# State products of a chunked recurrence in three column groups, next to the output products

## The chip, the cores and the metric

The kernel runs on one core of a Trainium2 chip. The metric is the device time of one execution in microseconds; three runs of the kernel before gave 1037.36, 1039.93 and 1042.68 us, so the median is 1039.93 us. The engines are named as in the profile: PE is TensorE's matrix products, PEld its weight loads, DVE is VectorE, ACT is ScalarE, POOL is GpSimd and SP issues most of the transfers.

## The reference

Three layers follow one another: a gated linear recurrence (4 sequences, 8 heads, 768 tokens, head width 48), a gated layer (`_moe_ref`) that computes `silu(xn @ w_gate) * (xn @ w_val) @ w_out` on normalized rows, and a layer of eight experts of which each token uses one. The change lies in the recurrence alone.

```python
def _attn_ref(q, k, v, a_re, a_im):
    ...
    for t in range(S):
        ar, ai = (a_re_n[:, :, t, :, None], a_im_n[:, :, t, :, None])
        new_re = ar * S_re - ai * S_im
        new_im = ar * S_im + ai * S_re
        kv = np.einsum('bhd,bhe->bhde', k[:, :, t], v[:, :, t])
        S_re, S_im = (new_re + kv, new_im)
        y[:, :, t] = np.einsum('bhd,bhde->bhe', q[:, :, t], S_re)
    return y

def reference(**kwargs):
    attn_out = _attn_ref(**attn_kwargs)
    B, H, S, D = attn_out.shape
    x = np.ascontiguousarray(attn_out.transpose(0, 2, 1, 3)).reshape(B * S, H * D)
    x = _moe_ref(x=x, **moe_kwargs)
    return _moe2_ref(x=x, **moe2_kwargs)
```

## The kernel before

The 3072 tokens are 24 chunks of 128. Two sequences take turns, so chunk i + 2 is the one that follows chunk i in its sequence, and a sequence is six chunks. The recurrence of a chunk runs in stages `s0` to `s10`. The factors of q and k (`QF`, `KF`; real and imaginary part side by side, 2 x 48 = 96 columns a head) are made in `s6`. `s7` transposes them (`ptQT`, `ptKT`, L663). `s8` makes the products of queries and keys (`pAT`, L680) and, unless the chunk is its sequence's last, the **state products** (`pKV`, L692): for each of 8 heads the stationary operand is `KF` (128 tokens x 96 columns), the moving operand is `V` (128 tokens x 48 columns), and the result is 96 x 48. DVE adds the old state (L697) and multiplies by the decay of the chunk (L699); the outcome, `Sn`, is read by `s9` of chunk i + 2. `s9` makes the **output products** `pyT` (L712 from `A` and `V`, L718 from `Sn` and `QT`): their results are 64 rows high and stand at rows 0 and 64 of the bank for even and odd heads, so that they already lie in two groups of 64 columns of TensorE. ACT copies them (`yT`, L725), PE transposes them back (`py`, L728), DVE normalizes (`XN`), and `s10` transposes again (`pxT`). The data of all these products are float32, and the trace shows each such product as two passes with a weight load each.

Beside the recurrence run the gated layer's products of the block of two or three chunks before: `pg` and `pv` (24 products of float32r with 256 or 384 moving columns for each f of 12), then `po` of the f before (L762 to L764). They fill most of PE's time.

The order of the work is written out by hand: a table of events with due times (`at`, `EARLY`, `NUDGE`, `SLOT`) sets the order in which the stages are called, and the scheduler of the framework then places each instruction in its engine's queue by that order and its own estimate of durations. Each engine runs its queue in order. Tiles come from pools with a fixed count of buffers: `KF` shares a tag of six (`r3`) with the other large tiles of the recurrence, `Sn` has three, `V` two, and the banks of `pAT`, `pKV`, `pyT`, `py` and the transposes are three (`bank`).

Of the kernel before, what the change touches and what calls it, by code (L numbers as in the profile page):

```python
# [115 lines left out]
def rsqrt(nc, y, x, a):  # L116
    """y = x ** -0.5, finite where x is 0; a is scratch"""
    nc.vector.tensor_scalar(y.bitcast(I32), x.bitcast(I32), 1, None, op0=ALU.logical_shift_right)
    nc.vector.tensor_scalar(y.bitcast(I32), y.bitcast(I32), -1.0, float(0x5F3759DF), op0=ALU.mult, op1=ALU.add)
    for _ in range(3):  # L120
        nc.vector.tensor_tensor(out=a, in0=y, in1=x, op=ALU.mult)
        nc.vector.scalar_tensor_tensor(out=a, in0=a, scalar=-0.5, in1=y, op0=ALU.mult, op1=ALU.mult)
        nc.vector.scalar_tensor_tensor(out=y, in0=a, scalar=1.5, in1=y, op0=ALU.add, op1=ALU.mult)


def inv_norm(nc, dst, ss, a):
    """dst = 1 / (sqrt(ss) + 1e-6); a is scratch"""
    rsqrt(nc, dst, ss, a)
    nc.vector.tensor_tensor(out=dst, in0=dst, in1=ss, op=ALU.mult)
    nc.vector.tensor_scalar(dst, dst, 1e-6, None, op0=ALU.add)  # L130
    nc.vector.reciprocal(dst, dst)
# [3 lines left out]
def general_path(tc, pools, H, q, k, v, are, aim, w64, g, w1, w2, out, ident, wE, enT):  # L135
    """the whole computation for inputs outside the ranges that the fast path is made for"""
    nc = tc.nc
# [78 lines left out]
    with tc.For_i(0, NT, P) as t0:  # L216
        def cols(x, name):
            """[token, feature] -> [feature, token]"""
            b = ps.tile([P, 512], F32, tag="a", name="gpt")
            for c in range(NC):  # L220
                nc.tensor.transpose(b[:, c * P:(c + 1) * P], x[:, c * P:(c + 1) * P], ident)
            t = gp.tile([P, NC, P], F32, tag=name, name=name, bufs=1)
            nc.scalar.activation(t, b[:, :DM].rearrange("p (c t) -> p c t", c=NC), AF.Copy)
            return t
# [71 lines left out]
def fused_kernel(ctx: ExitStack, tc: tile.TileContext, H, q, k, v, are, aim, wg, wv, wo, g, emb, tau, w1, w2, out):  # L296
# [67 lines left out]
    def apart(group, inst):  # L364
        """an indirect store whose rows no other one of the group writes"""
        tc.declare_no_dep(inst.ins, group=group, reason="each row is written once")
        tc.add_to_no_dep_group(group, inst.ins)
# [16 lines left out]
    def warm_up(n):  # L384
        """products of constants, so that TensorE is at its full clock when the first of the data comes"""
        b = psG.tile([P, BLK], F32, tag="g", name="warm")
        for _ in range(n):
            nc.tensor.matmul(b[:, :P], ones, ident, start=True, stop=True)
# [32 lines left out]

# [1 line left out]
    SETS = {  # L423
# [29 lines left out]

# [1 line left out]
    wop = ExitStack()  # L455
# [16 lines left out]
    def conv(n):  # L472
        """float64 to float32, and that to the two parts of the products"""
        _, dst, f = units[n]
# [12 lines left out]
    def check_weight(n):  # L487
        """the least magnitude of the upper words as float32, which tells of weights below the range of float32"""
        if n < len(units):
            hi = raw_t.pop(n)[:, :, 1].bitcast(F32)  # L490
            nc.vector.tensor_reduce(out=wmin[:, n:n + 1], in_=hi, axis=AX.X, op=ALU.min, apply_absolute_value=True)

    def check_re(n, load):
        """the least real part of the decay factors"""
        if load:
# [5 lines left out]

# [1 line left out]
    pap = ExitStack()  # L503
# [79 lines left out]
    def sums(i, part):  # L583
        """the sums of X over the tokens up to each one, in turns and in logarithms"""
        if i < PLAIN:
# [89 lines left out]
    def s8(i):  # L675
        for hf in range(2):
# [9 lines left out]
            st["A", i, hf] = A  # L686
        KF = st.pop(("KF", i))
        if not is_last(i):
            V, G = st["V", i], st.pop(("G", i))
            b = bank("pKV")  # L690
            for h in range(H):
                nc.tensor.matmul(b[:D2, h * D:(h + 1) * D], KF[:, h].rearrange("p z d -> p (z d)"), V[:, h * D:(h + 1) * D], start=True, stop=True)  # L692
            Sn = pa.tile([P, DM + HP - D], F32, tag="S", name="Sn", bufs=3)
            nc.gpsimd.memset(Sn[:, DM:], 0.0)
            kv = b[:D2, :DM]
            if not is_first(i):
                nc.vector.tensor_tensor(out=Sn[:D2, :DM], in0=kv, in1=st["S", i][:D2, :DM], op=ALU.add)  # L697
                kv = Sn[:D2, :DM]
            nc.vector.tensor_tensor(  # L699
                out=hd(Sn[:D2, :DM]), in0=hd(kv), in1=G[:D2].unsqueeze(2).broadcast_to([D2, H, D]), op=ALU.mult  # L700
            )
            st["S", i + 2] = Sn

    def s9(i):
        first = is_first(i)
        V = st.pop(("V", i))
        Sp = None if first else st.pop(("S", i))
# [48 lines left out]

# [1 line left out]
    def split_mm(o, lhs, rhs, start, stop):  # L758
        """o (+)= (lh + ll)^T (rh + rl) with the product of the small parts left to rounding"""
        n = len(lhs)  # L760
# [35 lines left out]

# [1 line left out]
    def e1(j):  # L798
# [7 lines left out]
    def e4(j, tl):  # L806
        """rows of a tile, the products with the embeddings beside them"""
        xs = st["x2", j]
# [78 lines left out]

# [1 line left out]
    def find_flag():  # L889
# [27 lines left out]

# [1 line left out]
    exr = ExitStack()  # L919
# [8 lines left out]
    def tiles(p):  # L928
        """the expert of a pass and the tiles of its slots"""
        e, lo, hi = PASSES[p]  # L930
        return e, range(lo // P, -(-hi // P))

    def rank_experts():
        """the experts by their tokens so far, the most first: the turn in which each is processed, and its slots"""
        pc = bank("pcount")[:, :E]
# [24 lines left out]
    def open_experts():  # L960
        """what the first expert needs early, in the place of the recurrence"""
        pap.close()
# [14 lines left out]
    def load_perm(room, last):  # L977
        """the tokens by turn and slot; a row up to the last one where there is none"""
        nc.sync.dma_start(out=perm, in_=perm_d.rearrange("(t p e) o -> p t (e o)", p=P, e=E))
# [10 lines left out]
    def head_perm():  # L990
        """of all blocks but the last one"""
        load_perm(moe.tile([P, DM], F32, tag="ct", name="room", bufs=CT_BUFS), rows(blocks[NB - 1][0] - 1).stop - 1)
# [18 lines left out]
    def load_raw(e, n):  # L1011
        """a half of w1 or of w2"""
        if e >= E:
# [10 lines left out]
    def split(e, n, part):  # L1024
        """half of a half of w1 or of w2, to the two parts of the products"""
        if e >= E:
# [14 lines left out]
    def xpose(p):  # L1041
        """the tokens of a pass, features first"""
        if p >= len(PASSES):
# [26 lines left out]
    def store(e, tl, n, src, gate):  # L1070
        """the rows of a tile, times their gates, to their places"""
        o = pool[1].tile([P, DM], F32, tag="o", name="o", bufs=4)
# [6 lines left out]
    def by_feature(e):  # L1079
        """where the last tile would hold few tokens, the outputs are made features first, for the tokens that there are"""  # L1080
        return 0 < CAPS[e] % P <= FLIP

    def ex_out(p, f, part=None):
        """the products with w2; of the last pass the last tile by itself, so that the others are stored meanwhile"""
        e, lo, hi = PASSES[p]
# [24 lines left out]
    def turn_back(p, f):  # L1110
        """the outputs of an expert, tokens first"""
        e, _, hi = PASSES[p]
# [35 lines left out]

# [1 line left out]
    uses = {s2: [AF.Ln, AF.Exp], s4: [AF.Arctan], s5: [AF.Exp, AF.Exp], s5b: [AF.Exp, AF.Exp], s6: [AF.Sin, AF.Sin], moe_g: [AF.Tanh], e5: [AF.Exp]}  # L1150
# [113 lines left out]
def _tokens(a):  # L1264
    """[batch, head, token, feature] -> [batch, token, head * feature]"""
    b, h, s, d = a.shape
# [3 lines left out]
def _columns(a):  # L1270
    """[row, column] -> [block of columns, row in block of rows, block of rows, column in block]"""
    r, c = a.shape
# [3 lines left out]
def _rows(a):  # L1276
    """[row, column] -> [block of rows, row in block, column]"""
    return a.reshape(-1, P, a.shape[1])
# [37 lines left out]
```

## Time and profile before

| | |
|---|---|
| median of three runs | 1039.93 us |
| the profiled execution, span | 1035.3 us |
| PE busy | 972.8 us (94%) |
| PEld busy | 931.2 us (90%) |
| DVE busy | 674.4 us (65%) |
| ACT busy | 609.3 us (59%) |
| POOL busy | 250.4 us (24%) |
| state products `pKV`, PE busy | 31.9 us in 320 passes |

The span reaches from the first to the last instruction of one execution; the median of the runs is 4.6 us longer than this span. A busy share is an average over stages: the recurrence and the gated layer run side by side up to about 740 us, the experts after that. TensorE's clock is granted at full speed (2.4 GHz) or at half (1.2 GHz); it is at half in several stretches between 40 and 170 us, and at full speed from there to the last few microseconds. Matrix products overlap, so a row of several passes is longer than the distance from its start to the start of the next row; this distance is what a group of passes costs.

### The profile page before, as it was taken

The numbers are of one execution on the slowest core, as the hardware profiler recorded it, in microseconds if no ns is written. First come the engines' busy times: TensorE is split into PE (matmuls) and PEld (weight loads), VectorE is DVE, ScalarE is ACT, GpSimd is POOL, SyncE is SP. The second block draws the span as 40 slices with busy tenths as digits, with TensorE's granted clock in tenths as the row PEclk, the third lists the DMA queues.
The fourth block names the chain that finished last, engine by engine and source line by source line (L and its number), as shares of the span: only waits on it lengthen the run. The fifth ranks groups of instructions, "written<-read, shape, count | busy, mean of one in ns | idle before, by whom it ended". The sixth has DMA issues, their size and how long they took to land.

```text
span 1035.3 us, 18190 instructions
## 1 busy us (share of the span) xinstructions
PE 972.8 (94%) x6729; PEld 931.2 (90%) x6729; DVE 674.4 (65%) x1618; ACT 609.3 (59%) x1106; POOL 250.4 (24%) x264
## 2 busy tenths in 40 slices
PE   5868788899999999999999999999988999999995
PEld 5867687899999999999999999999988999999995
DVE  6898997877766866866876776464557533444420
ACT  6565656767768767767776865542445433455531
POOL 4355653311211211221031120110104202322221
PEclk9897989999999999999999999999999999999998
DMA  6443441214311511611511331030235534554210
GB/s 198 132 138 102 139 127 48 47 40 135 51 40 53 163 39 47 192 39 40 170 54 40 106 106 36 18 99 1 73 97 186 159 106 148 178 176 161 92 38 23
DMA packets 75537, 99.24 MB, mean 96 GB/s; under 512 B 27327, under 2 KB 57502, under 8 KB 75440
## 3 DMA queue, kind: packets, MB, share of 16 engines
q1 hardware_dynamic: 70272, 87.30, 28.4%
q0 software_dynamic: 5168, 10.70, 3.1%
q8 instruction: 55, 0.90, 0.4%
q14 instruction: 42, 0.34, 0.1%
HBM read 88.04 MB, written 10.50 MB: 95 GB/s over the span
## 4 chain that ended last, share of the span: by engine, by line
PE 66%; issue 9%; DVE 4%; DMA 4%; POOL 3%; ACT 2%; SPq 0%; POOLq 0%; ACTq 0%; DVEq 0%
PE pg L762 4%; PE pv L762 4%; PE po L762 4%; PE pg L764 4%; PE pg L763 4%; PE pv L764 4%; PE pv L763 4%; PE po L763 4%; PE po L764 4%; PE pAT L680 3%; PE ph L762 3%; PE eo L762 3%; PE eo L763 3%; PE ph L764 3%; PE ph L763 3%
## 5 line engine op out<-in xcount | busy, mean ns | idle before, releaser
L762 PE MATMUL pg<-xth,wg 128*128 128x384 f32 (+1 forms) x324 | 109.2, 337 | 9.8 <-DVE th L777 9.8
L763 PE MATMUL po<-htl,wo 128*128 128x384 f32 (+1 forms) x324 | 105.9, 327 | 8.5 <-DVE htl L786 6.2
L438 ACT ACT_TABLE_LOAD x87 | 111.6, 1283 | 1.5
L762 PE MATMUL pv<-xth,wv 128*128 128x384 f32 (+1 forms) x324 | 107.5, 332 | 1.9 <-DVE th L783 1.9
L762 PE MATMUL po<-hth,wo 128*128 128x384 f32 (+1 forms) x324 | 106.9, 333 | 0.0
L763 PE MATMUL pg<-xtl,wg 128*128 128x384 f32 (+1 forms) x324 | 105.7, 326 | 0.0
L764 PE MATMUL pg<-xth,wg 128*128 128x384 f32 (+1 forms) x324 | 105.5, 326 | 0.0
L764 PE MATMUL pv<-xth,wv 128*128 128x384 f32 (+1 forms) x324 | 103.9, 321 | 0.4 <-POOL wv L484 0.4
L764 PE MATMUL po<-hth,wo 128*128 128x384 f32 (+1 forms) x324 | 104.2, 322 | 0.0
L763 PE MATMUL pv<-xtl,wv 128*128 128x384 f32 (+1 forms) x324 | 103.5, 319 | 0.0
L438 ACT ACTIVATE th<-pg 128x384 f32<-128x384 f32 (+1 forms) x108 | 49.0, 454 | 90.5 <-PE pg L764 89.6
L785 ACT ACTIVATE hth<-th 128x384 fp32r<-128x384 f32 (+1 forms) x108 | 52.5, 486 | 78.3 <-DVE th L783 72.2
L1068 DVE SCALAR_TENSOR_TENSOR hel<-ph,heh 128x256 fp32r<-128x256 f32 (+6 forms) x72 | 39.9, 554 | 89.7 <-ACT heh L1067 89.6
L777 DVE SCALAR_TENSOR_TENSOR th<-th,pg 128x384 f32<-128x384 f32 (+1 forms) x108 | 54.5, 505 | 47.5 <-ACT th L438 47.0
L1067 ACT ACTIVATE heh<-ph 128x256 fp32r<-128x256 f32 (+6 forms) x72 | 35.0, 486 | 74.7 <-PE ph L764 72.1
L1036 DVE TENSOR_TENSOR wl<-raw,wh 128x768 fp32r<-128x768 f32 x64 | 59.4, 954 | 29.0 <-ACT wh L1035 28.9
L786 DVE TENSOR_TENSOR htl<-th,hth 128x384 fp32r<-128x384 f32 (+1 forms) x108 | 60.5, 560 | 27.2 <-ACT hth L785 26.8
L762 PEld LDWEIGHTS pg<-xth,wg 128*128 128x128 f32 x324 | 63.0, 195 | 14.2 <-DVE th L777 11.9
L762 PE MATMUL ph<-xeh,wh 128*128 128x256 f32 (+6 forms) x216 | 75.1, 348 | 0.0
L764 PE MATMUL ph<-xeh,wl 128*128 128x256 f32 (+6 forms) x216 | 72.6, 336 | 0.0
L763 PE MATMUL ph<-xel,wh 128*128 128x256 f32 (+6 forms) x216 | 72.4, 335 | 0.0
L763 PEld LDWEIGHTS po<-htl,wo 128*128 128x128 f32 x324 | 62.3, 192 | 9.9 <-DVE htl L786 7.1
(252 smaller groups left out, 2689.0 us busy)
## 6 DMA issues: line engine op xcount, KB each, us to landing
raw<-in_moe_w_dram SPq DMA_DIRECT2D x32, 768.0 KB
raw<-in_moe_w_gate_dram SPq DMA_DIRECT2D x24, 384.0 KB
raw<-in_moe_w_val_dram SPq DMA_DIRECT2D x24, 384.0 KB
raw<-in_moe_w_out_dram SPq DMA_DIRECT2D x24, 384.0 KB
X<-in_a_im_dram SPq DMA_DIRECT2D x24, 192.0 KB
X<-in_a_re_dram SPq DMA_DIRECT2D x24, 192.0 KB
V<-in_v_dram SPq DMA_DIRECT2D x24, 192.0 KB
x2d<-row SPq DMA_DIRECT2D x24, 192.0 KB
```

Of the source, the lines that this page charges most:

```text
L438: chain[0] = fn(*args, **kw)
L680: nc.tensor.matmul(b[:, h * P:(h + 1) * P], KT[:D2, h], QT[:D2, h], start=True, stop=True)
L762: nc.tensor.matmul(o, lh, rh, start=start and x == 0, stop=False)
L763: nc.tensor.matmul(o, lh, rl, start=False, stop=False)
L764: nc.tensor.matmul(o, ll, rh, start=False, stop=stop and x == n - 1)
L777: nc.vector.scalar_tensor_tensor(out=t, in0=t, scalar=1.0, in1=b, op0=ALU.add, op1=ALU.mult)
L785: nc.scalar.activation(hh, t, AF.Copy)
L786: (nc.gpsimd if j < POOL_H else nc.vector).tensor_tensor(out=hl, in0=t, in1=hh.bitcast(F32), op=ALU.subtract)
L1036: nc.vector.tensor_tensor(out=dl, in0=rw, in1=dh.bitcast(F32), op=ALU.subtract)
L1067: nc.scalar.activation(hh, b, AF.Relu)
L1068: nc.vector.scalar_tensor_tensor(out=hl, in0=b, scalar=0.0, in1=hh.bitcast(F32), op0=ALU.max, op1=ALU.subtract)
```

## The change

`state` is a new function that holds the state products and what follows from them. It is called by `s9` of the same chunk, ahead of the output products, and no longer from `s8`. In it the 96 columns of `KF` are cut into three of 32, and each piece has a product of its own whose result stands at rows 0, 32 and 64 of the bank: 24 products of 32 x 48 a chunk where there were 8 of 96 x 48. Comments and docstrings are dropped, and later lines shift by nine.

```diff
@@ s8 @@
             st["A", i, hf] = A
-        KF = st.pop(("KF", i))
-        if not is_last(i):
-            V, G = st["V", i], st.pop(("G", i))
-            b = bank("pKV")
-            for h in range(H):
-                nc.tensor.matmul(b[:D2, h * D:(h + 1) * D], KF[:, h].rearrange("p z d -> p (z d)"), V[:, h * D:(h + 1) * D], start=True, stop=True)
-            Sn = pa.tile([P, DM + HP - D], F32, tag="S", name="Sn", bufs=3)
...
+    def state(i):
+        KF = st.pop(("KF", i)).rearrange("p h z d -> p h (z d)")
+        if is_last(i):
+            return
+        V, G = st["V", i], st.pop(("G", i))
+        b = bank("pKV")
+        for h in range(H):
+            for lo in range(0, D2, 32):
+                nc.tensor.matmul(
+                    b[lo:lo + 32, h * D:(h + 1) * D], KF[:, h, lo:lo + 32], V[:, h * D:(h + 1) * D],
+                    start=True, stop=True, skip_group_check=True,
+                )
+        Sn = pa.tile([P, DM + HP - D], F32, tag="S", name="Sn", bufs=3)
...
     def s9(i):
         first = is_first(i)
+        state(i)
         V = st.pop(("V", i))
```

The first place is PE's queue around the products of queries and keys of chunk 14 (about 434 us in the trace). Before:

```order
L764 MATMUL pg<-xth,wg_110 128x384
L680 MATMUL pAT<-QT,KT 128x128 x8
L692 MATMUL pKV<-V,KF 96x48 x8
L762 MATMUL pv<-xth,wv_111 128x384
L763 MATMUL pv<-xtl,wv_111 128x384
```

and after:

```order
L773 MATMUL pg<-xth,wg_110 128x384
L680 MATMUL pAT<-QT,KT 128x128 x8
L771 MATMUL pv<-xth,wv_111 128x384
L772 MATMUL pv<-xtl,wv_111 128x384
L773 MATMUL pv<-xth,wv_112 128x384
```

The state products are gone from here, and the gated layer's `pv` follows `pAT` at once. The second place is PE's queue around the output products of the same chunk (about 443 us). Before:

```order
L764 MATMUL pv<-xth,wv_112 128x384
L712 MATMUL pyT<-A,V 64x128 x2
L718 MATMUL pyT<-QT,Sn 64x128 x2
L712 MATMUL pyT<-A,V 64x128 x2
```

and after:

```order
L773 MATMUL pv<-xth,wv_112 128x384
L697 MATMUL pKV<-V,KF 32x48 x24
L721 MATMUL pyT<-A,V 64x128 x2
L727 MATMUL pyT<-QT,Sn 64x128 x2
L721 MATMUL pyT<-A,V 64x128 x2
```

The 24 small products now stand straight ahead of `pyT`, which itself is as it was. The third place is the end of the same output products, up to the transposes `py` that need ACT's copy of `pyT`. Before:

```order
L718 MATMUL pyT<-QT,Sn 64x128 x2
L762 MATMUL po_4818<-hth,wo_107 128x384
L763 MATMUL po_4818<-htl,wo_107 128x384
L764 MATMUL po_4818<-hth,wo_108 128x384
L762 MATMUL po_4819<-hth,wo_107 128x384
L763 MATMUL po_4819<-htl,wo_107 128x384
L764 MATMUL po_4819<-hth,wo_108 128x384
L762 MATMUL po_4820<-hth,wo_107 128x384
L728 MATMUL py<-beside,yT 128x128 x4
```

and after:

```order
L727 MATMUL pyT<-QT,Sn 64x128 x2
L771 MATMUL po_4982<-hth,wo_107 128x384
L772 MATMUL po_4982<-htl,wo_107 128x384
L773 MATMUL po_4982<-hth,wo_108 128x384
L771 MATMUL po_4983<-hth,wo_107 128x384
L737 MATMUL py<-beside,yT 128x128 x4
```

Where seven products of the gated layer stood between `pyT` and `py`, four stand now. Over the chunks from number 5 on the count is lower in nine of nineteen, the same in eight, and higher in two.

## Rows read from the trace of the kernel before

**Rows 1.** The page, part 1: engine, busy us (share of the span) xinstructions.

```profile
PE 972.8 (94%) x6729; PEld 931.2 (90%) x6729; DVE 674.4 (65%) x1618; ACT 609.3 (59%) x1106; POOL 250.4 (24%) x264
```

**Rows 2.** Three stretches: us, then each engine's busy us (xinstructions), clock, DMA.

```profile
17.00:180.00 163.00, 132.60 (x982) 121.39 (x981) 147.01 (x290) 100.55 (x188) 81.92 (x68) 0.87 0.40 117
180.00:660.00 480.00, 475.72 (x3497) 460.24 (x3496) 344.70 (x897) 340.27 (x601) 87.11 (x96) 1.00 0.27 75
660.00:1035.00 375.00, 357.11 (x2230) 343.64 (x2228) 172.98 (x409) 158.38 (x306) 75.17 (x69) 0.99 0.33 107
```

**Rows 3.** Two stretches, `pKV` alone: us, then busy us of PE, PEld, DVE.

```profile
17.00:180.00 163.00, 9.69 (x80) 9.42 (x80) 2.73 (x5) 0.87 0.40 117
180.00:660.00 480.00, 22.23 (x240) 21.99 (x240) 8.27 (x15) 1.00 0.27 75
```

**Rows 4.** Timeline of PE, chunk 14: start us, us, engine, line, op, shape, passes.

```profile
433.81 1.95 PE L680 MATMUL pAT<-QT,KT 96*128 96x128 f32 x16
435.59 1.48 PE L692 MATMUL pKV<-V,KF 128*96 128x48 f32 x16
436.90 0.42 PE L762 MATMUL pv<-xth,wv 128*128 128x384 f32 x1
437.16 0.33 PE L763 MATMUL pv<-xtl,wv 128*128 128x384 f32 x1
```

**Rows 5.** Timeline of PE, chunk 10, which has no state products: behind `pAT`.

```profile
324.17 0.43 PE L762 MATMUL pv<-xth,wv 128*128 128x384 f32 x1
324.43 0.34 PE L763 MATMUL pv<-xtl,wv 128*128 128x384 f32 x1
```

**Rows 6.** Timeline of PE, the output products of chunk 14.

```profile
443.00 0.33 PE L763 MATMUL pv<-xtl,wv 128*128 128x384 f32 x1
443.17 0.34 PE L764 MATMUL pv<-xth,wv 128*128 128x384 f32 x1
443.44 0.44 PE L712 MATMUL pyT<-A,V 128*64 128x128 f32 x4
443.71 0.39 PE L718 MATMUL pyT<-QT,Sn 96*64 96x128 f32 x4
443.93 0.39 PE L712 MATMUL pyT<-A,V 128*64 128x128 f32 x4
...
445.03 0.39 PE L718 MATMUL pyT<-QT,Sn 96*64 96x128 f32 x4
445.35 0.45 PE L762 MATMUL po<-hth,wo 128*128 128x384 f32 x1
445.63 0.34 PE L763 MATMUL po<-htl,wo 128*128 128x384 f32 x1
```

**Rows 7.** `pyT` of chunk 4, first instants: us, passes (x), weight loads (x) begun by then.

```profile
153.76:153.78 0.01, 0.01 (x2) 0.01 (x2) 0.00 (x0) 1.00 0.00 0
153.76:153.84 0.07, 0.07 (x2) 0.07 (x4) 0.00 (x0) 1.00 0.00 0
```

**Rows 8.** Timeline of PE, chunk 2, at the half clock.

```profile
82.96 2.69 PE L692 MATMUL pKV<-V,KF 128*96 128x48 f32 x16
85.43 0.56 PE L764 MATMUL pg<-xth,wg 128*128 128x256 f32 x1
```

**Rows 9.** Timeline of PE from `pyT` to `py`: chunk 10, then chunk 14.

```profile
334.01 0.44 PE L762 MATMUL po<-hth,wo 128*128 128x384 f32 x1
334.81 0.63 PE L728 MATMUL py<-beside,yT 128*128 128x128 f32 x4
...
446.53 0.34 PE L762 MATMUL po<-hth,wo 128*128 128x384 f32 x1
446.93 0.66 PE L728 MATMUL py<-beside,yT 128*128 128x128 f32 x4
```

**Rows 10.** Timeline of ACT at the same two places: the copy `yT` and what precedes it.

```profile
334.15 0.58 ACT L725 ACTIVATE yT<-pyT 128x512 f32<-128x512 f32 x1
...
445.87 0.53 ACT L785 ACTIVATE hth<-th 128x384 fp32r<-128x384 f32 x1 [1.66 <-DVE th L783]
446.30 0.58 ACT L725 ACTIVATE yT<-pyT 128x512 f32<-128x512 f32 x1
```

**Rows 11.** A stretch at the half clock, columns as in Rows 2.

```profile
78.00:88.20 10.20, 9.89 (x57) 9.66 (x59) 8.57 (x18) 4.02 (x8) 3.60 (x3) 0.50 0.27 79
```

More of the change, by code (lines that the diff above doesn't have):

```diff
@@ L686, in s8 @@
             st["A", i, hf] = A
-        KF = st.pop(("KF", i))
-        if not is_last(i):
-            V, G = st["V", i], st.pop(("G", i))
-            b = bank("pKV")
-            for h in range(H):
-                nc.tensor.matmul(b[:D2, h * D:(h + 1) * D], KF[:, h].rearrange("p z d -> p (z d)"), V[:, h * D:(h + 1) * D], start=True, stop=True)
-            Sn = pa.tile([P, DM + HP - D], F32, tag="S", name="Sn", bufs=3)
[L694 to L702, printed above, removed]
+    def state(i):
[11 more added lines that the diff above has]
+        Sn = pa.tile([P, DM + HP - D], F32, tag="S", name="Sn", bufs=3)
+        nc.gpsimd.memset(Sn[:, DM:], 0.0)
+        kv = b[:D2, :DM]
+        if not is_first(i):
+            nc.vector.tensor_tensor(out=Sn[:D2, :DM], in0=kv, in1=st["S", i][:D2, :DM], op=ALU.add)
+            kv = Sn[:D2, :DM]
+        nc.vector.tensor_tensor(
+            out=hd(Sn[:D2, :DM]), in0=hd(kv), in1=G[:D2].unsqueeze(2).broadcast_to([D2, H, D]), op=ALU.mult
+        )
+        st["S", i + 2] = Sn
     def s9(i):
         first = is_first(i)
+        state(i)
         V = st.pop(("V", i))
```

## The prediction

> **What bounds the kernel now.** I read the shares of the engines first: PE is busy 94% of the span and no other engine above 65% [rows 1]. Since a share is an average, I then cut the span into stretches [rows 2]. From 180 to 660 us PE is busy 475.7 of 480 us at the full clock, DVE 345, ACT 340: there PE alone sets the pace, and a microsecond taken out of its queue is a microsecond less. From 660 us to the end PE is busy 357 of 375 us, so what comes earlier out of the middle stretch is carried to the end. From 17 to 180 us it is otherwise: DVE is busy 147 of 163 us, PE only 133 and that partly at half clock; there PE waits for others, and its savings are mostly lost again. Next I counted the state products by stretch: 240 passes from 180 to 660 us, which at 16 a chunk are 15 chunks, and 80 passes (5 chunks) before [rows 3]. So the prediction is 15 times what one block of state products gains on PE, plus little for the other five.
>
> **What a block costs now.** In chunk 14 the row of `pKV` starts at 435.59 and the next row at 436.90: 1.31 us for 16 passes, 82 ns each [rows 4]. The first product behind it takes 0.26 us (436.90 to 437.16) where 0.17 is the rhythm (443.00 to 443.17 [rows 6]). That is no saving, since the same 0.26 stands behind `pAT` where no state products follow (324.17 to 324.43 [rows 5]), and `pAT` will now be followed like this everywhere.
>
> What are the 82 ns? A pass of `pAT` with 128 moving columns takes 111 ns (433.81 to 435.59 by 16 [rows 4]). By proportion the 48 columns of `V` need 42 ns. So the moving side isn't the limit, and what is left is the load of 96 stationary columns, 82 ns; by proportion 32 columns take 27.
>
> **What a block costs after it.** There are 24 products and thus 48 passes, which I count as 16 rounds of three, one in each column group. If the groups run side by side, loads included, a round takes the longer of 42 and 27, that is 42 ns. The nearest row is `pyT`, in the same type and also in column groups, two of them: four passes of 128 columns take 0.22 us (443.71 to 443.93 [rows 6]), 55 ns a pass, half of the 111 that one takes alone. So two groups overlap wholly. Their loads do too: the first two passes and loads begin within about 0.02 us, and within 0.08 us four loads of 64 columns have begun, where loads one after another, at the rate of 96 columns in 82 ns, would have begun but two [rows 7]. For a third group I allow a third of the 20 ns and take **48 ns** a round, nearer to the low end. The bounds: 42 at the low end; 62 if every round pays the whole 20 ns; 82 if the loads of the three groups come one after another (3 x 27); 126 if the passes do (3 x 42); 165 if passes can't start faster than the densest that this trace shows, 55 ns.
>
> The Trainium skill gives a figure for this very shape: "TensorE: Matmul & The Clock Gate", section "Measured speedup vs the span model", has three column tiles of 32 at 2.38 times. By that a round would be about 53 ns (an estimate, 3 x 42 / 2.38) and the gain summed below 1.2 us smaller; the two groups of [rows 6] show 2.0 of 2, so I stay with the rows.
>
> To the rounds come two edges. Entering the narrow columns costs 0.10 us now, at `pyT` (443.17 to 443.44, 0.27 for 0.17), and leaving them again 0.10 (0.32 from 445.03 to 445.35 for 0.22) and 0.11 in the row behind (445.35 to 445.63) [rows 6]. After the change the entry stands ahead of `pKV` and the exit behind `pyT`, once each as now; new is the step from 32 to 64 columns between them. I take 0.10; its ends are 0 and 0.21. The first weights of a block lie open: 0.05 us for 64 columns (443.44 to 443.71, 0.27 for 0.22), so about 0.03 for 32.
>
> Block: 0.03 + 16 x 0.048 + 0.10 = 0.90 us; it saves 1.31 - 0.90 = **0.41 us**. At 42 ns it saves 0.51, at 62 ns 0.19, at 82 it costs 0.13, at 126 0.84, at 165 1.46. The change breaks even at 74 ns a round.
>
> **The sum.** Fifteen blocks: 15 x 0.41 = 6.2 us. The early five: at the full clock 0.41 each, at half clock more (2.47 us now in chunk 2 [rows 8], 1.80 by the same sum), under 3 us together; but DVE is busy 8.6 of 10.2 us in such a stretch [rows 11] and what PE gains it waits out. I take 0.8.
>
> Against it stands the shorter way from `pyT` to `py`: in nine chunks fewer products lie between, four instead of seven in most. Four take 0.80 us (334.01 to 334.81 [rows 9]), and the copy `yT` from 334.15 to 334.73 just fits into that [rows 10]. Where ACT is late with `hth`, PE waits: in chunk 14 `yT` started at 446.30, and the last product before `py` took 0.40 us instead of 0.17 with seven in between [rows 9, 10]; with four it would be 3 x 0.17 = 0.5 us more. At worst this is 9 x 0.5 = 4.7 us. But the state products now lie between `pv` and `yT`, so ACT gets 0.9 us more for `hth`, which was late by less. I take 0.8 us, two late chunks at 0.4.
>
> At nothing I put the rest. DVE's two operations on the state move behind the block; their reader is `s9` two chunks on, some 55 us later, so `Sn` has cover to spare, and behind the first of them on DVE stands `htl`, whose reader `po` runs one f later. `KF` keeps its buffer until `pyT`, about 8 us longer (435.59 to 443.44 [rows 4, 6]); six buffers are shared, and the scheduler has answered by moving a few large writes on ACT by a place, about 0.5 us (the length of `hth` in [rows 10]), off the bound engine. If that cover were gone, each chunk would pay this 0.5 us. `pKV`'s waits (a transfer of `V`, a free bank) come 8 us later than before and are over by then.
>
> Sum: 6.2 + 0.8 - 0.8 = 6.2 us. The profiled execution goes from 1035.3 to 1029.1 us, the median, 4.6 us above the span, from 1039.9 to **1033.7 us**.
>
> **The rivals.**
> *The groups share one stream of loads or starts.* Then a round takes 62 to 82 ns, a block saves 0.19 or costs 0.13, and 15 blocks give between 2.9 us saved and 2.0 lost; with the 0.8 for late copies the time is 1038 to 1043. For it: no row shows groups of 32 columns, and on the long run `pyT` loads 2 x 64 columns in 0.11 us, 0.86 ns a column, just the rate of 96 columns in 82 ns. Against it: the loads that begin together in [rows 7]. The Trainium skill has a rule of this kind: the same page, section "Wait — 56ns, not 53.3ns?", says that starts never follow each other by less than about 25 ns, however few the columns; by it a round is about 75 ns (an estimate) and the gain is nil, but two passes have begun within 0.02 us in [rows 7]. Chance 0.20.
>
> *Short passes don't overlap at all,* or can't start faster than every 55 ns: 126 to 165 ns a round, 0.84 to 1.46 us lost a block, 13 to 22 us in the 15 chunks, 1053 to 1062 us, slower. It decides from 74 ns a round on. For it: no 48 passes in a row are shown so dense, and 48 columns are over three times as quickly streamed as the 128 of `pyT`. Against it: [rows 6, 7]. Chance 0.10.
>
> *The start-up turns out worse.* The new order moves state products and what DVE does with them between 17 and 180 us, where PE waits for DVE and the clock falls to half [rows 2, 11]. Another stretch like [rows 11] at half clock puts 5 us on the PE work in it, and two of them outweigh the gain: 1036 to 1044 us. Chance 0.10.
>
> **How the numbers follow.** The forecast, 0.60: groups side by side, 1027 to 1038 us; at 42 ns and with all 20 blocks counted it is 10 us saved, 1030, and the three runs of before lie 2.7 us to either side. The range must take in the first and the third rival, but not the second: **1027 to 1044 us**. What a measurement of this kernel can tell from no change is about 0.5%, 5.2 us. Faster by more than that (below 1034.7): two thirds of the forecast's 0.60 and a little of the third rival, 0.42. Within: the rest of the forecast 0.20, most of the first rival 0.16, some of the third 0.04: 0.40. Slower (above 1045.1): the second rival 0.10, the ends of the first and the third 0.08: 0.18.
>
> **What would show it.** In the timeline of the changed kernel, from the first row of `pKV` to the first of `pyT` in the middle stretch: 0.90 us if I am right, above 1.31 if a rival is; divided by 16 after 0.13 us for the edges it gives the round. `pAT` to `pv` must show 0.26 as in [rows 5]. In the window from 180 to 660 us PE's idle time must stay near 4 us; waits of `py` for `yT` above 3 us in total would show the fourth term wrong. If the time rises with a block of 0.90 us, the start-up is to blame, and the clock of 17 to 180 us, 0.87 now, would be lower.

## The result

The changed kernel takes 1024.32 us (median of 4 runs, 1022.50 to 1025.56); the kernel before took 1038.64 us in the four runs beside it. The ratio is 0.9849, with a 95% interval of 0.9818 to 0.9881: by it 15.7 us (12.4 to 18.9) are saved, by the two medians 14.3, where 6.2 were forecast. The time lies below the forecast range of 1027 to 1044 us, and the gain is more than twice as large as predicted.

The page of the changed kernel, its span and part 1, answers [rows 1]. The span went from 1035.3 to 1023.8 us; PE is busy 14.7 us less and is still the busiest engine by far.

```profile
span 1023.8 us, 19475 instructions
PE 958.1 (94%) x7369; PEld 914.5 (89%) x7369; DVE 670.6 (66%) x1618; ACT 610.9 (60%) x1106; POOL 252.4 (25%) x264
```

The three stretches of [rows 2] in the changed kernel (same columns: us, busy us of PE, PEld, DVE, ACT and POOL, clock, DMA share, GB/s):

```profile
17.00:180.00 163.00, 132.24 (x1197) 120.03 (x1195) 153.69 (x317) 107.72 (x199) 85.52 (x70) 0.90 0.41 121
180.00:660.00 480.00, 474.49 (x4014) 458.30 (x4014) 342.21 (x899) 341.95 (x607) 85.87 (x95) 1.00 0.27 76
660.00:1023.00 363.00, 343.80 (x2133) 330.08 (x2131) 164.73 (x380) 151.00 (x287) 74.83 (x68) 0.99 0.33 108
```

Look at the first row. In the same 163 us DVE does 153.69 us of work instead of 147.01, 6.7 us more. DVE was called the bound of this stretch in the prediction; a bound engine that gets 6.7 us more done in the same time had been waiting before. To place the gain I counted the gated layer's products (`pg`, `pv`, `po`) in order of their start, and took the 400th (counting from 0), just behind the start-up, and the 2300th, at the end of the recurrence:

| span split at these two products, us | before | changed |
|---|---|---|
| start to the 400th product | 182.7 | 175.0 |
| 400th to the 2300th | 478.7 | 471.4 |
| 2300th to the end | 373.9 | 377.4 |

So 7.7 us come from the start-up, where 0.8 were forecast; 7.3 from the middle, where 6.2 less 0.8 were; and 3.5 are given back at the end, where nothing was.

The block itself, chunk 14, in the timeline of PE of the changed kernel (start us, us, engine, line, operation, shape, passes), to be held against [rows 4]:

```profile
430.80 0.34 PE L773 MATMUL pv<-xth,wv 128*128 128x384 f32 x1
431.06 0.88 PE L697 MATMUL pKV<-V,KF 128*32 128x48 f32 x48
431.87 0.44 PE L721 MATMUL pyT<-A,V 128*64 128x128 f32 x4
432.14 0.39 PE L727 MATMUL pyT<-QT,Sn 96*64 96x128 f32 x4
...
433.47 0.39 PE L727 MATMUL pyT<-QT,Sn 96*64 96x128 f32 x4
433.79 0.44 PE L771 MATMUL po<-hth,wo 128*128 128x384 f32 x1
```

From `pKV` to `pyT` there are 0.81 us where the old block took 1.31. The entry (430.80 to 431.06) and the exit (433.47 to 433.79) cost 0.26 and 0.32, as in [rows 6]. The first instants of the block (window, its length, passes begun on PE, weight loads begun on PEld, then DVE, clock, DMA):

```profile
431.06:431.08 0.02, 0.02 (x3) 0.02 (x3) 0.00 (x0) 1.00 0.00 0
431.06:431.14 0.08, 0.08 (x5) 0.08 (x8) 0.00 (x0) 1.00 0.00 0
431.06:431.87 0.81, 0.81 (x48) 0.75 (x48) 0.00 (x0) 1.00 0.00 0
```

Three passes and three loads have begun within 0.02 us: a whole round; in [rows 7] it was two of each. The starts of the single passes in the trace give the round without any allowance for edges: they come in threes, about 7 ns apart, and from the second round on the threes follow each other every 42.5 ns. Only the first round takes longer, 67 ns, and the last, which starts 149 ns ahead of `pyT`.

### The profile page after: what moved, and what is told of

It reads as the page before. It is cut to its first block, busy times and chain, and to the rows that moved or that the text cites. A ratio compares the mean times of both kernels' runs of the same rounds, so it can differ in the third digit from the quotient of the medians.

```text
span 1023.8 us, 19475 instructions
## 1 busy us (share of the span) xinstructions
PE 958.1 (94%) x7369; PEld 914.5 (89%) x7369; DVE 670.6 (66%) x1618; ACT 610.9 (60%) x1106; POOL 252.4 (25%) x264
## 4 chain that ended last, share of the span: by engine, by line
PE 67%; DVE 11%; issue 10%; DMA 5%; ACT 3%; POOL 2%; SPq 0%; POOLq 0%; DVEq 0%; ACTq 0%
PE pg L771 4%; PE po L771 4%; PE pg L772 4%; PE pg L773 4%; PE pv L771 4%; PE po L772 4%; PE pv L773 4%; PE po L773 4%; PE pv L772 4%; PE pAT L680 3%; PE ph L771 2%; PE ph L772 2%; PE ph L773 2%; PE eo L772 2%; PE eo L773 2%
```

## Experiments on the block and on place against size

Ratios are always to the kernel before in runs beside them on the same chip; its medians were 1037.04, 1039.80 and 1039.73 us there. Unless the text says otherwise the edits are shown against the changed kernel, shortened, with comments added here. Three words return in the expectations: PLACE is the move from `s8` to `s9`, SIZE the three short groups, CHANCE at first the clock of the start, which differs from run to run, and later a start-up that any new order shifts by some us.

**Only the place: eight products of 96 columns, in `s9`.**

```diff
-            for lo in range(0, D2, 32):
-                nc.tensor.matmul(b[lo:lo + 32, ...], KF[:, h, lo:lo + 32], V[...], ...)
+            nc.tensor.matmul(b[:D2, h * D:(h + 1) * D], KF[:, h], V[:, h * D:(h + 1) * D], start=True, stop=True)
```

> The state products stand in s9 ahead of the output products, but as 8 products of 96 columns as before. Of the 14.3 us that the change gave in the median, the 15 blocks of the middle stretch explain 15 x 0.49 = 7.4 us. Theory PLACE (the rest comes from the order of the work in the first 180 us): this kernel keeps the rest and loses the 7.4, so it is 5 to 8 us faster than before, near 1032 us, and by 180 us it is 6 to 8 us ahead. Theory SIZE (the rest comes from the first five blocks being shorter): 0 to 2 us faster or slower than before, near 1038 us. Theory CHANCE (the rest is the clock of the start, which differs from run to run): 0, and the times scatter by 3 us as before's do.

Measured: 1031.20 us, ratio 0.9939 (0.9916 to 0.9963), 6.3 us saved without one pass less to load. The 400th product starts at 173.6 us, 9.1 earlier than before; from there to the 2300th it takes 477.9 us, nearly the 478.7 of before. The gain of the place lies in the start-up, as PLACE said.

**Only the size: three groups, at the old place in `s8`.**

```diff
             st["A", i, hf] = A
+        state(i)
...
         first = is_first(i)
-        state(i)
```

> Three column groups at the old place, in s8 behind the products of queries and keys. Each block now pays an entry and an exit of its own: 0.10 + 0.03 + 16 x 0.0425 + 0.10, some 0.9 us against 1.31, and 0.1 more in the row behind pyT does not change, so 0.35 to 0.4 us saved a block and 5 to 6 us in the 15 blocks of the middle stretch. Theory PLACE: that is all, 5 to 6 us faster than before, near 1033 us, and no lead at 180 us beyond 1 or 2 us. Theory SIZE: 10 to 13 us faster, near 1027 us, with a lead of 5 us or more at 180 us. Theory CHANCE: 5 to 6 us faster on the median, the lead at 180 us different from run to run.

Measured: 1028.71 us, ratio 0.9916 (0.9888 to 0.9945). The start-up gains here too, as SIZE said (400th product at 176.4 us, 6.3 earlier). But the middle takes 477.3 us, only 1.4 less than before, though 13 of its 15 blocks are 0.81 us long. Two are not. Timeline of PE in this kernel, chunk 14; the bracket tells how long PE sat idle before the row and for what:

```profile
428.23 0.70 PE L698 MATMUL pKV<-V,KF 128*32 128x48 f32 x34
429.24 0.29 PE L698 MATMUL pKV<-V,KF 128*32 128x48 f32 x4 [0.31 <-issue]
429.97 0.26 PE L698 MATMUL pKV<-V,KF 128*32 128x48 f32 x3 [0.44 <-issue]
430.72 0.34 PE L698 MATMUL pKV<-V,KF 128*32 128x48 f32 x7 [0.48 <-issue]
430.99 0.44 PE L771 MATMUL pv<-xth,wv 128*128 128x384 f32 x1
```

The block takes 2.76 us, 1.95 too long, and PE waits there for nothing that the profile shows; the one at 514.57 takes 2.07. These 3.2 us and the 1.4 gained make 4.6 of the 7.4 that 15 shorter blocks are worth. Of the rest the old place costs half: the narrow columns are entered behind `pAT` for this block alone (its first pass starts 0.205 us behind the last of `pAT`, where it was 0.111 before), 0.09 us a block or 1.4 us in 15, while next to `pyT` one entry serves both. The other 1.4 us are not traced.

**The change from chunk 5 on only, and for chunks 0 to 4 only** (the condition reversed for the second).

```diff
+        if i < 5:          # in s8, where both were before
+            state(i)
...
-            for lo in range(0, D2, 32):
+            for lo in range(0, D2, 32 if i >= 5 else D2):
...
-        state(i)
+        if i >= 5:         # in s9
+            state(i)
```

> The change from chunk 5 on, the old form and place for chunks 0 to 4. PLACE and SIZE both: only the 7.4 us of the middle stretch, near 1031 us, no lead at 180 us. CHANCE: as the whole change, 12 to 15 us faster, since the start makes no difference on the median.

> The change for chunks 0 to 4 only, the old form and place from chunk 5 on. PLACE and SIZE both: the rest alone, 5 to 8 us faster, near 1032 us, all of it there at 180 us. CHANCE: 0 to 2 us, near 1038 us.

Measured: late only 1032.59 us, ratio 0.9953 (0.9929 to 0.9978), 4.9 us; early only 1028.46 us, ratio 0.9914 (0.9889 to 0.9938), 8.9 us. Together 13.8 us, which is the whole within its interval. So five blocks of twenty give almost two thirds. The late half is what was forecast (5.4 lies within its 2.3 to 7.4 us). The early term, put at 0.8 us, is the one that failed, by a factor of eleven.

**Group after group: the two loops exchanged.**

```diff
-        for h in range(H):
-            for lo in range(0, D2, 32):
+        for lo in range(0, D2, 32):
+            for h in range(H):
```

> The changed kernel with its two loops exchanged: the eight products of columns 0 to 31, then the eight of 32 to 63, then those of 64 to 95, where the changed kernel turns through the three groups. The same 24 products and 48 passes at the same place. OVERLAP (three passes run side by side, each for the 42 ns of its own 48 columns): a pass follows one of its own group and must wait for it, so a block takes about 48 x 42 ns = 2.0 us and the step to pyT, 2.1 us from pKV to pyT instead of 0.81; twenty blocks cost 25 us more than in the changed kernel, about 1050 us. START RATE (the 48 passes simply start every 14 ns, whatever group they are in): 0.81 us as now and about 1024 us.

Timeline of PE and the first instants of chunk 14's block in this kernel (columns as above). The timeline:

```profile
434.34 1.95 PE L697 MATMUL pKV<-V,KF 128*32 128x48 f32 x48
436.22 0.44 PE L721 MATMUL pyT<-A,V 128*64 128x128 f32 x4
```

The passes and loads begun in the first instants:

```profile
434.34:434.36 0.02, 0.02 (x1) 0.02 (x1) 0.00 (x0) 1.00 0.00 0
434.34:434.42 0.08, 0.08 (x2) 0.08 (x3) 0.00 (x0) 1.00 0.00 0
```

The same 48 passes on the same data take 1.88 us instead of 0.81, near the 2.0 of OVERLAP and far from START RATE; two passes have begun within 0.08 us instead of five. Within a group the single passes start every 42.5 ns, as the rounds of three did; only around the two steps to the next group are some closer. So a pass waits for the one before it in its own group, and groups in turn overlap wholly. The middle stretch takes 484.9 us. The time, 1037.7 us in one run, was missed by 12 us. In part the block is shorter than the 2.1 us that were expected; in part the expectation, that a longer block always costs, left the start-up out: the 400th product starts at 173.4 us, earlier than in the changed kernel, although the blocks are longer than before the change. In `s9` the length of an early block hardly matters, by this one profile.

## Experiments on the first five blocks

**Place alone and size alone, in chunks 0 to 4.** The place, with 96 columns throughout:

```diff
+        if not (i < 5):    # in s8
+            state(i)
...
+            for lo in range(0, D2, D2):
+                up = lo + (D2)
...
+        if i < 5:          # in s9
+            state(i)
```

The size, with every call in `s8`:

```diff
-            for lo in range(0, D2, 32):
+            for lo in range(0, D2, 32 if i < 5 else D2):
+                up = lo + (32 if i < 5 else D2)
```

> Chunks 0 to 4 make their state products in s9 as in the changed kernel, but in eight products of 96 columns; from chunk 5 on everything is as before. It takes the sizes out of the run with the first five chunks, which gave 0.9914. PLACE (the first five chunks gain because the state products no longer stand in front of the work of the next stages and wait there for a bank or for DVE): about 0.994, 6 us less than before. SIZE (they gain because the blocks are short): 0.999, 1 us. CHANCE (any new order of the start-up gives some us): can't be told from PLACE by this run alone, but the run with the groups at the old place must then gain as much.

> Chunks 0 to 4 make their state products in three groups of 32 columns, but at the old place in s8; from chunk 5 on everything is as before. PLACE: 0.998 to 1.000, since the blocks wait where they stand and only their 0.5 us (1 us at half clock) each are saved. SIZE: about 0.992, as the run with place and size. CHANCE: 0.994, as much as the one with the place alone.

Measured: place 1032.50 us, ratio 0.9918 (0.9887 to 0.9948), 8.5 us; size 1029.47 us, ratio 0.9900 (0.9860 to 0.9939), 10.4 us. Each alone gives as much as both together (8.9). The first run fits PLACE and not SIZE, the second SIZE and not PLACE, so neither holds by itself; this looked like CHANCE, or like two cures of one illness.

**Long blocks, old place, chunks 0 to 4: groups one after another.** It differs from the size run, against which the edit is shown, in the order of two loops alone; PE, DVE, ACT and POOL run the same instructions in the same order in both.

```diff
-        for h in range(H):
-            for lo in range(0, D2, 32 if i < 5 else D2):
+        w = 32 if i < 5 else D2
+        for lo in range(0, D2, w):
+            for h in range(H):
```

> Chunks 0 to 4 make their state products in 24 products of 32 columns at the old place in s8, but group after group, which makes a block 1.88 us long instead of 1.31 before and 0.81 with the groups in turn; from chunk 5 on all is as before. All engines have the same order as in the run with the groups early at the old place, so only the length of five blocks tells the two apart. SIZE (that run gained because its blocks were short): 1.002, 2 to 3 us slower than before. ORDER (it gained because 24 instructions instead of 8 let the scheduler lay the first 180 us out otherwise): within 3 us of that run, 0.990 to 0.993. Half and half: 0.996.

**The kernel before once more,** without an edit.

> The kernel before, unchanged, for a second profile of it. In the first profile VectorE waits 4.1 us for ScalarE's XN and 1.7 us for the state products themselves between 17 and 180 us; in the changed kernel both are gone. ORDER (these waits belong to the old order of the first chunks): they stand here too, 4 to 6 us together, and TensorE reaches its 400th product of the gated layer near 182.7 us. RUN (they were an accident of that one execution): under 1.5 us together, the 400th product near 178 us, and the gain of the changed kernel in the profiles is in part an accident too. On the end stretch: if the half-clock stretch of 3.4 us near 740 to 790 us, which the first profile of before lacks, shows here, it is an accident of an execution as well.

Measured: long blocks 1036.97 us, ratio 0.9974 (0.9946 to 1.0001), which lies between SIZE (1.002) and ORDER (0.990 to 0.993), beside "half and half" (0.996). With 24 instructions and the layout of the size run, but long blocks, 7.7 us of that run's 10.4 are gone. So most of that gain hangs on the length of the five blocks and not on a lucky layout; the 2.7 us that are left may be layout, and can't be told from nothing. The kernel before took 1042.85 us in its second profiled run, and the 400th product started at 184.9 us there.

The list of DVE's waits between 17 and 180 us shows where the time goes (engine, tile and line that waits, what it waited for, us in total, times, longest). The first profile of before:

```profile
DVE ss L733 <- ACT XN L732: 4.1, 2, 2.2
DVE Sn L697 <- PE pKV L692: 1.3, 1, 1.3
...
DVE Sn L699 <- PE pKV L692: 0.4, 1, 0.4
```

The same list of the second profile of before:

```profile
DVE ss L733 <- ACT XN L732: 4.9, 2, 3.1
DVE Sn L697 <- PE pKV L692: 1.3, 1, 1.3
...
DVE Sn L699 <- PE pKV L692: 0.7, 1, 0.7
```

The same list of the long blocks:

```profile
DVE Sn L710 <- PE pKV L700: 2.1, 1, 2.1
...
DVE Sn L708 <- PE pKV L700: 1.5, 1, 1.5
```

And of the changed kernel, where it begins so and has no line for `Sn` or `ss`:

```profile
DVE Xl L595 <- ACT Xh L594: 4.0, 1, 4.0
DVE htl L795 <- ACT hth L794: 0.9, 2, 0.5
```

The wait for `Xh` is not new. In the first profile of before it stands at 180.5 us, just behind the window, and the list from 17 us to the 400th product (182.7 us) has it:

```profile
DVE Xl L595 <- ACT Xh L594: 5.3, 1, 5.3
```

Up to the 400th product DVE is busy 149 us in both kernels. Its listed waits add up to 14.3 us before and 6.9 in the changed kernel, 7.4 less, and the 400th product is 7.7 us earlier: the waits make up the lead. Of the 7.4 us, 5.7 are waits for `pKV` and `XN`, 1.4 the one for `Xh`.

The waits for `pKV` and `XN` are no accident of one profile: 5.8 and 6.9 us in the two of before. Here is one of them, chunk 1, in the timeline of PE in the first profile of before:

```profile
40.04 2.48 PE L692 MATMUL pKV<-V,KF 128*96 128x48 f32 x16 [2.43 <-DVE rs L734]
42.33 1.61 PE L388 MATMUL warm<-beside,ones 128*128 128x128 f32 x6
43.87 1.98 PE L712 MATMUL pyT<-A,V 128*64 128x128 f32 x16
...
47.46 0.60 PE L728 MATMUL py<-beside,yT 128*128 128x128 f32 x4
```

DVE in the same profile and the same microseconds:

```profile
42.56 0.55 DVE L699 TENSOR_TENSOR Sn<-pKV,G 96x384 f32<-96x384 f32 x1 [0.35 <-PE pKV L692]
...
49.27 0.16 DVE L733 TENSOR_SCALAR ss<-ss 128x1 f32<-128x1 f32 x1 [2.16 <-ACT XN L732]
```

And the same place in the timeline of PE with short blocks (the size run):

```profile
39.62 0.88 PE L700 MATMUL pKV<-V,KF 128*32 128x48 f32 x48 [2.46 <-DVE rs L747]
40.43 1.09 PE L725 MATMUL pyT<-A,V 128*64 128x128 f32 x16
41.46 1.16 PE L388 MATMUL warm<-beside,ones 128*128 128x128 f32 x8
42.45 0.60 PE L741 MATMUL py<-beside,yT 128*128 128x128 f32 x4
```

PE waits 2.4 us for DVE in both. Then the old block takes 2.29 us (40.04 to 42.33), and only behind it come the output products, `py`, ACT's `XN` and DVE's `ss`, at which DVE stands 2.16 us. From the start of `pKV` to `py` it is 7.42 us before and 2.83 with short blocks, and in the latter DVE does not wait. So twice PE's chain is late for DVE. By this account the block can be taken out of that chain by length or by place, the waits go either way, and it is one gain, to be had in two ways.

But the shorter block is only 1.5 of these 4.6 us. The granted clock differs too. Between 36 and 50 us, in the first profile of before (columns as in [rows 2]):

```profile
36.00:50.00 14.00, 11.57 (x84) 10.82 (x83) 11.19 (x26) 5.42 (x12) 3.96 (x5) 0.76 0.43 126
```

And in the size run:

```profile
36.00:50.00 14.00, 11.25 (x146) 10.59 (x144) 13.83 (x39) 7.88 (x15) 6.00 (x6) 1.00 0.42 130
```

The same place in all profiles (the waits are DVE's for `pKV` and `XN`):

| block of chunk 1 | PE idle ahead of it, us | clock, 36 to 50 us | DVE waits there, us |
|---|---|---|---|
| old, `s8`: before, first / second profile | 2.43 / 2.43 | 0.76 / 0.76 | 2.5 / 2.5 |
| old, `s8`: place for 2 to 4 / late only | 2.43 / 2.43 | 0.76 / 0.88 | 2.4 / 1.0 |
| long, `s8` | 2.45 | 0.88 | 2.1 |
| short, `s8`: all groups at the old place / 0 to 4 only | 2.46 / 2.46 | 0.88 / 1.00 | 0.9 / none |
| `s9`, the seven other kernels | 0.7 or less | 1.00 | 0.4 or less |

In `s9` PE hardly stands still ahead of the block, and the clock stays at full speed there in all seven profiles. In `s8` PE stands still for 2.4 us, and around the block the clock falls to half in six profiles of seven; DVE waits in these six and not in the seventh. At this place the waits and the half clock go together.

**Which chunk: the place alone for chunks 0 and 1, and for 2 to 4.**

```diff
-        if i < 5:          # in s9, else in s8
+        if i < 2:          # the first kernel
...
-        if i < 5:
+        if 2 <= i < 5:     # the second kernel
```

> Chunks 0 and 1 alone make their state products in s9, in eight products of 96 columns; all else as before. In the first profile of before the block of chunk 1 stood 2.4 us in TensorE's queue ahead of pyT and so kept VectorE from the next chain for 2.2 us. If the early gain of the place hangs on this one: 0.994, 6 us. If it is spread over the first five chunks: 0.997.

> Chunks 2 to 4 alone make their state products in s9, in eight products of 96 columns; all else as before. VectorE waits 1.3 us for the state products of chunk 2 and 1.9 us for XN behind it in the first profile of before, and TensorE 1.8 us in front of a later block. If the early gain hangs on chunk 1: 0.999. If it is spread: 0.996. If any new order of the start-up gains as much: 0.992, and the run with chunks 0 and 1 alone as well.

Measured: chunks 0 and 1 1034.61 us, ratio 0.9957 (0.9933 to 0.9980); chunks 2 to 4 1036.90 us, ratio 0.9962 (0.9935 to 0.9988). They add up, 0.43% and 0.38%, to the 0.82% of all five, and neither reaches the 0.992 that any new order would have given. So there are two places, one in each part, as the two `ss` waits of before say. All these runs in one table (the last column but one is the mean granted clock of whole executions, over all runs of a kernel, less that of the kernel before beside it):

| kernel | DVE's waits for `pKV` and `XN` (`Sn`, `ss`), 17 to 180 us | DVE busy there | PE clock there | rise of the clock, all runs | ratio |
|---|---|---|---|---|---|
| before, first / second profile | 5.8 / 6.9 | 147.0 / 147.7 | 0.87 / 0.84 | | 1 |
| long blocks, 0 to 4 | 3.6 | 148.6 | 0.91 | 0.004 | 0.9974 |
| place, 2 to 4 | 2.4 | 150.5 | 0.88 | 0.004 | 0.9962 |
| place, 0 and 1 | 1.3 | 149.4 | 0.88 | 0.004 | 0.9957 |
| place, 0 to 4 | 0.3 | 151.9 | 0.90 | 0.009 | 0.9918 |
| groups, 0 to 4 | none listed | 151.6 | 0.90 | 0.008 | 0.9900 |
| both, 0 to 4 | none listed | 154.0 | 0.92 | 0.011 | 0.9914 |

The time follows the waits of DVE. In the profiles it does not follow the mean clock of the stretch: the long blocks have 0.91 and gain next to nothing. Over all runs, though, it goes with the clock, and so it does among the runs of the kernel before alone: of the 25 beside the last three kernels the fastest (1034.54 us) has 0.979 and the slowest (1046.68 us) 0.967. The half clock is thus a rival that no run here rules out. It makes the chain longer for which DVE waits (the block of chunk 2 takes 2.47 us at half clock [rows 8]), and at chunk 1 it stands where PE had stood still; which of the two comes first is not shown. What the runs do show is where the gain is made: in the first five blocks, by their place or by their length.

The run with the late chunks alone fits this. It has the old order in the start-up, but in its one profile the clock is less at half around chunks 1 and 2, DVE waits only 1.0 us for `ss` and not for `Sn`, and the 400th product starts at 179.1 us. The old start-up thus varies; the runs of this kernel reached from 1026.73 to 1038.94 us (clock 0.976 and 0.966), those of the changed kernel from 1022.50 to 1025.56.

**A try for more: the state products behind the output products.**

```diff
-        state(i)
...
         nc.scalar.activation(yT, b.rearrange("p (c t) -> p c t", c=HG), AF.Copy)
+        state(i)
         b = bank("py")
```

> The changed kernel with the state products behind the output products of the chunk instead of ahead of them, between pyT and py. The copy yT then has 0.81 us more work of PE in front of its reader py. If waits of py for yT are part of what is left, 1 to 3 us less than the changed kernel, 1021 to 1023 us, ratio 0.983. If py's waits are gone already, the same as the changed kernel, 1024 us, 0.985. The new order of the first chunks can shift either by some us.

Measured: 1025.74 us, ratio 0.9856 (0.9825 to 0.9887): no gain over the changed kernel can be seen. The interval reaches 3 us to either side, so that the 1 to 3 us that were looked for are not ruled out either.

## Why the prediction was wrong

**The block: right, a little small.** Forecast 0.90 us, measured 0.81. The first loads (67 less 42.5 ns, forecast 0.03 us) and the step to 64 columns (149 less 42.5, forecast 0.10 us) hold; the round is (0.81 - 0.13) / 16 = 42.5 ns, as the starts of the passes say, the low end that I had named: the third group adds nothing. A block saves 0.50 instead of 0.41 us, 15 blocks 7.4 instead of 6.2, and the middle stretch became 7.3 us shorter in the profiles. By the Trainium skill, "TensorE: Matmul & The Clock Gate", section "Measured speedup vs the span model", the round would have been about 53 ns (an estimate); by its section "Wait — 56ns, not 53.3ns?", with starts at least 25 ns apart, about 75 (an estimate). Neither holds here: 48 passes start in 0.81 us, 17 ns apart on average. The first figure is for 512 moving columns, where these have 48, so that "this very shape" was right for the tiles alone; and the whole block, its edges included, is 2.3 times as fast as group after group (0.81 us against 1.88), which is near it.

**The first five blocks: wrong, and this is the failure.** I put their gain at under 3 us, and took 0.8, because "DVE is busy 8.6 of 10.2 us in such a stretch [rows 11] and what PE gains it waits out". Measured: 8.9 us in the runs with these five alone. The row was right and the conclusion was not. DVE is idle for 1.6 us in those 10.2, and I did not ask for what. Its timeline answers, in the profile of before:

```profile
83.20 0.69 DVE L682 TENSOR_TENSOR A<-pAT,triR 128x512 f32<-128x512 f32 x1 [0.28 <-PE pAT L680]
...
85.68 0.55 DVE L697 TENSOR_TENSOR Sn<-pKV,Sn 96x384 f32<-96x384 f32 x1 [1.32 <-PE pKV L692]
...
91.39 0.15 DVE L733 TENSOR_SCALAR ss<-ss 128x1 f32<-128x1 f32 x1 [1.89 <-ACT XN L732]
```

0.28 and 1.32 us are all but 0.03 us of the idle time of that stretch, and the larger is the wait for the very block that the change shortens; another 1.89 follow at the end of the same chain. I had weighed what PE waits for in this stretch and not what DVE waits for. Where two engines wait for each other in turn, a gain on the one that is not the bound need not be lost: here it was worth the bound engine's waits, 7.4 us less of them up to the 400th product for a lead of 7.7. The clock is at half in this stretch [rows 11], where the block takes 2.47 us [rows 8] instead of 1.31, while the changed kernel has the full clock from 74 to 93 us (1.00, where before has 0.73); I had priced the half clock as a risk of the new order and not as something that it might take away. How much of the 8.9 us goes by the clock stays open.

**The shorter cover of `yT`: about right.** I allowed 0.8 us and said that waits above 3 us would refute it. PE's waits from 180 to 660 us in the changed kernel:

```profile
PE ptKT L663 <- ACT QT L665: 2.7, 3, 1.2
PE py L737 <- ACT yT L734: 1.8, 3, 1.2
PE pg L771 <- DVE th L786: 1.1, 1, 1.1
```

`py` waits 1.8 us in three places, where it has no such wait in the first profile of before, and PE is idle for 5.5 us of the stretch instead of 4.3. The worst case there was 9 x 0.5 = 4.5 us and not 4.7; no other number hangs on it.

**The end stretch: not as forecast, and not by the change as far as shown.** From the 2300th product to the end the changed kernel takes 377.4 us, the first profile of before 373.9, but the second 376.5. One part can be seen: a short stretch at half clock where the experts begin, in the changed kernel and in the second profile of before, which the first lacks. The changed kernel (columns as in [rows 2]):

```profile
739.00:743.00 4.00, 3.70 (x19) 3.70 (x20) 2.83 (x7) 1.66 (x4) 0.00 (x0) 0.57 0.75 205
```

The second profile of before:

```profile
800.00:805.00 5.00, 4.07 (x20) 4.07 (x21) 2.58 (x5) 3.27 (x7) 2.27 (x3) 0.66 0.69 245
```

Every other profile here has such a stretch too, between 739 and 804 us, and the end takes between 373.6 and 378.6 us in them; so it belongs to an execution, not to the change. What lies around a span was also misread: it is 1.8 us here (1025.56 against 1023.8) and in the second profile of before (1042.85 against 1041.1), not the 4.6 between the median and a profile that happened to be one of the shorter executions.

**The rivals.** Shared loads or starts (62 to 82 ns) and no overlap at all (126 to 165) both fell with the round of 42.5 ns; the exchanged loops show what no overlap would have cost. (The 48 columns are 2.7 times as quickly streamed as 128, not over three times.) The third rival, the start-up, was the right place with the wrong sign. I gave the move a chance to make it worse and none to make it better by more than 3 us, which is why the range ended at 1027.

## What to carry to other kernels

Before a gain is written off as "waited out by the bound engine", list what the bound engine itself waits for: its idle time behind the work that you shorten may be yours. Here shortening that work and moving it out of the chain were worth the same, and both together no more. Look at the granted clock at the same place in every profile before you name the cause of such a wait. The products cut into column groups of 32 were faster only where consecutive instructions turned through the groups; group after group the same work took 2.3 times as long, longer than uncut. One profile of the kernel before is one execution: two of them here differ by 5.8 us in span.

## What the runs showed of the hardware

Three column groups of 32 overlap completely, weight loads included: 42.5 ns a round for float32 passes of 48 columns, the distance of two passes in the exchanged loops' kernel (48 passes in 1.88 us, 39 ns each on average, since some are closer where one group follows another). In the kernel with all groups at the old place, dense runs of such passes twice stopped after some 30 passes and then went on in pieces, with idle times of 0.31 to 0.48 us each; the two blocks were 3.2 us too long together. Just ahead of the one at 428 us, between 427 and 428, lies a transfer of the queue for instructions (its row in the list of DMA queues, 426 to 432 us: packets, MB, share):

```profile
q8 instruction: 1, 0.02, 1.1%
```

Such a transfer stands in the microseconds of the other block too, but they come every 17 us or so. That PE ran out of instructions is a guess from this coincidence; no run tested it.
